# Threshold attention and an exact GELU MLP on one core: ten token blocks instead of eight by products of quarters, x^T copied by ScalarE and divided by GpSimd

## The chip, the cores and the metric

The kernel runs on one core of a Trainium2 chip. The engines of the core work side by side, each through its own list of instructions in order, and wait for one another by semaphores: TensorE (PE in the profile, with PEld for its weight loads) multiplies matrices into PSUM, VectorE (DVE) and ScalarE (ACT) work on tiles in SBUF and PSUM, GpSimd (POOL) works on tiles in SBUF and issues transfers, SyncE (SP) issues transfers. The metric is the time of one execution on the device in microseconds (us). Everything is float32; the weights arrive as 64-bit floats and are converted on the chip. What an engine computes is not changed by the edit beyond the order of some sums.

## The reference

There are 8 batches of 8 heads with 576 tokens of 64 elements. The attention keeps, in each row of scores, only those within tau of the row's maximum; a two-layer MLP follows.

```python
scores = scale * np.matmul(q, k.transpose(0, 1, 3, 2))
thresh = np.max(scores, axis=-1, keepdims=True) - tau
scores = np.where(scores >= thresh, scores, -1000000000.0)
scores = scores - np.max(scores, axis=-1, keepdims=True)
attn = np.exp(scores)
attn = attn / (np.sum(attn, axis=-1, keepdims=True) + 1e-09)
x = attn @ v                      # heads side by side: 4608 tokens x 512
h = x @ w_in                      # 512 x 2048
g = 0.5 * h * (1.0 + erf(h * inv_sqrt2))
out = g @ w_out                   # 2048 x 512
```

## The kernel before, in words

**Pairs and slots.** Two heads make a pair, four pairs a batch, 32 pairs in all. The 576 query rows of a pair are cut into four chunks of 128 rows for each of the two heads and a fifth chunk that holds the last 64 rows of both. One chunk is one slot: slots 0 to 3 of a pair have two score tiles (head 0 and head 1), slot 4 has one. Slots are numbered n = 0 to 159 through the kernel; the first 20 (the first batch) are done in another way and are not touched.

**One slot of the softmax.** `scores` (L358) has TensorE multiply q^T by k^T into a score tile in PSUM; the pool named sc has two such tiles, so that a slot with two tiles can only start when the slot before has let its own go. `softmax_head` takes the maximum with VectorE (L370, nmx), computes the threshold with GpSimd (L371, thr), and exponentiates with ScalarE (L373, p). `softmax_tail` has VectorE compare the score tile with the threshold, multiply, and sum the row (L389); this is the last reader of the score tile. `turn_p` (L436, L434) then has VectorE transpose p in 32x32 blocks, `regroup` has SyncE bring the blocks to their places in pT by DMA (L454, L458), and after slot 4 `divisors` inverts the row sums and has SyncE spread them over a tile named inv (L411 to L424).

**x^T.** In slot 2 of the next pair (`WEIGH = 2`) `weigh_v` multiplies v by p^T on TensorE into two tiles xT (L475, 20 matmuls in all), and VectorE multiplies xT by inv into a block of x, x_blk (L492). The function that does this, `divide`, is handed back to the main loop, which calls it for the first tile after `softmax_tail` and for the second after `turn_p`. In slot 2 VectorE also transposes q and k of the next pair (L340 to L346).

**The MLP as filling.** The 4608 tokens are 18 blocks of 256. A block done plainly (`block_steps`) is 64 matmuls of 256 columns for the first layer (hT, L549; after each eight, ScalarE applies GELU, L522, which needs a table load before it and one after it, L535, to get back to Exp) and 32 matmuls of 512 columns for the second (o_ps, L563). These matmuls are the filling that TensorE does in each slot behind the scores. How many go into a slot is fixed when the program is written out: `GOAL` gives the number of blocks that are to be done by certain slots, `PARTS = 1.2, 1.2, 0.8, 1.2, 0.6` shares it out over slots 0 to 4 of a pair, and `fill` emits matmuls until the debt is paid, from blocks whose tokens are ready (`tokens`).

**The blocks at the end.** The last 8 blocks are done two by two after the attention (`strassen`, L683): with seven products of quarters in place of eight, a duo of blocks takes 224 matmuls of 256 columns, where two plain blocks take 128 of 256 and 64 of 512 columns. VectorE makes the sums of quarters of w_in in `weights_in` (L623 to L631) and of x in `x_sums` (L649 to L652). Blocks that must wait for it and have no room in SBUF (`AWAY`) are written to DRAM by `put_away` and fetched by `bring`, both on SyncE's queue; the pool xg has seven buffers for blocks of x.

**GpSimd's list.** In slots 1 to 4 it holds, behind the slot's thr instructions, the issue of the loads of q, k and v of the pair after the next (four DMAs a slot, L224 and L233).

Of the kernel before, what the change touches and what calls it, by code (L numbers as in the profile page):

```python
# [8 lines left out]
FP32 = mybir.dt.float32  # L9
# [3 lines left out]
ALU = mybir.AluOpType  # L13
# [5 lines left out]
def kernel(  # L19
# [28 lines left out]
    nc = tc.nc  # L48
    ctx.enter_context(tc.manual_schedule())

    B, H, S, D = q.shape
    d_model, d_ff = moe_w_in.shape
    P = 128
    Q = 32
    HP = H // 2
    NP = B * HP
    EARLY = HP
# [6 lines left out]
    N_DM = d_model // P  # L64
    N_DF = d_ff // P
    TOK = 256
    N_BLK = B * S // TOK
    PLAIN = N_BLK - 8

    AWAY = [PLAIN, PLAIN + 1, PLAIN + 2]  # L70
    order = list(range(PLAIN + 3, N_BLK)) + AWAY
    DUOS = list(zip(order[0::2], order[1::2]))
    assert 2 * D == P and 2 * TAIL == P and HALF <= 512 and N_DM == HP and B * S % TOK == 0 and S % Q == 0 and TOK == 2 * P
    SLOTS = NC + 1
# [8 lines left out]
    xg = ctx.enter_context(tc.tile_pool(name="xg", bufs=7))  # L83
    op = ctx.enter_context(tc.tile_pool(name="op", bufs=2))
# [123 lines left out]
    st = {}  # L208
    x_blk = {}

    def load(p):
        for _ in load_steps(p):
            pass
# [135 lines left out]
    def scores(p, i):  # L349
        s = st[p]  # L350
        n = 1 if i == NC else 2
        sc = s["sc", i] = [ps.tile([P, 2, 512], FP32, tag="sc", name="sc", bufs=2) for _ in range(n)]
        for h in range(2):
            for e in range(n):
                rows = slice(0, P) if i == NC else slice(e * D, (e + 1) * D)
                lhsT = s["q_tail"] if i == NC else s["qT"][rows, i * P:(i + 1) * P]
                at = h * HALF + (TAIL if p < EARLY and e == 0 else 0)
                nc.tensor.matmul(  # L358
                    sc[e][:, h, 0:HALF], lhsT=lhsT, rhs=s["kT"][rows, at:at + HALF], start=True, stop=True)

    def softmax_head(p, i):

        s = st[p]
        n = len(s["sc", i])
        nmx = small.tile([P, 2], FP32, tag="nmx", name="nmx")
        thr = s["thr", i] = small.tile([P, 2], FP32, tag="thr", name="thr")
        w = s["p", i] = work.tile([P, 2 * S], FP32, tag="p", name="p")
        for e in range(n):
            sc = s["sc", i][e][:, :, 0:HALF]
            nc.vector.tensor_reduce(nmx[:, e:e + 1], sc, axis=AXIS.XY, op=ALU.max, negate=True)  # L370
            nc.gpsimd.tensor_scalar(  # L371
                thr[:, e:e + 1], nmx[:, e:e + 1], -1.0, tau_eff, op0=ALU.mult, op1=ALU.subtract)
            nc.scalar.activation(  # L373
                w[:, e * S:(e + 1) * S].rearrange("p (h s) -> p h s", h=2), sc, AF.Exp, bias=nmx[:, e:e + 1], scale=1.0)
# [64 lines left out]
    def by_64(t):  # L439
        return t.rearrange("p c s -> p (c s)").rearrange("p (g c s) -> p g c s", c=KR, s=2 * Q)  # L440
# [19 lines left out]
    def weigh_v(p, lo, hi):  # L460


        b, hp = divmod(p, HP)
        s = st[p]
        xT = ps.tile([P, 512], FP32, tag="mm", name="xT")
        for c in range(KR):
            for e in range(2):
                f = slice(e * D, (e + 1) * D)
                to = xT[f, 0:hi - lo]
                if p < EARLY:  # L470
                    rhs = s["pT"][0 if c == NC else e][:, c, lo:hi]
                else:
                    to = to.rearrange("p (g s) -> p g s", s=2 * Q)
                    rhs = by_64(s["pT"][e])[:, lo // (2 * Q):hi // (2 * Q), c, :]
                nc.tensor.matmul(  # L475
                    to, lhsT=s["v"][:, e, c, :], rhs=rhs, start=(c == 0), stop=(c == KR - 1))
        by = None if p < EARLY else s["inv"]
        if hi == S:
            del st[p]

        def divide():
            at = lo
            while at < hi:
                n, o = divmod(b * S + at, TOK)
                size = min(TOK - o, hi - at)
                if n not in x_blk:
                    x_blk[n] = xg.tile([P, N_DM, TOK], FP32, tag="x", name="x")
                to, x = x_blk[n][:, hp, o:o + size], xT[:, at - lo:at - lo + size]
                if by is None:
                    nc.scalar.copy(to, x)  # L490
                else:
                    nc.vector.tensor_tensor(to, x, by[:, at:at + size], op=ALU.mult)  # L492
                at += size

        if by is not None:
            return divide
        divide()


    NS_IN, NS_OUT = 4 * TOK / 2.4, 4 * d_model / 2.4  # L500
# [25 lines left out]
    def gelus_held():  # L526
        hold[0] = False
        while held:
            g, j, t = held.pop(0)
            gelu(g, j, t, t)  # L530
# [41 lines left out]
    def fill(ns, tokens):  # L572

        mlp["debt"] += ns
        while True:
            if mlp["next"] is None:
                n = mlp["n"]
                if n == PLAIN or (n + 1) * TOK > tokens:
                    break
# [32 lines left out]
    def weights_in():  # L612
# [13 lines left out]

        assert mlp["n"] == PLAIN and mlp["layer"] == 2
        for h in range(HF // U):
# [173 lines left out]
    BATCH = HP * SLOTS  # L802
    WIDE = 5 * 2 * Q
    WEIGH = 2
    START = 2 * HP + 2

    GOAL = [(-1, 0.0), (START - 1, 0.0), (BATCH - 1, 0.5)]
    GOAL += [(BATCH * (m + 2) + WEIGH, x) for m, x in enumerate([1.96, 3.3, 4.64, 5.98, 7.32, 8.66, PLAIN])]

    def goal(n):  # L810
        for (lo, x), (hi, y) in zip(GOAL, GOAL[1:]):
# [11 lines left out]
    loads = iter(())  # L823
    for n in range(len(slots) + WEIGH + 1):
        p, i = slots[n] if n < len(slots) else divmod(n, SLOTS)
        early = p < EARLY
        last = slots[n - 1] if 0 < n <= len(slots) else None
        if p < NP:
            scores(p, i)
            softmax_head(p, i)  # L830
        elif n == len(slots):
            ext = weights_in()
        gelus(0)
        if n == BATCH:
            gelus_held()
        table()
        made = []
        for args in due:
            weigh_v(*args)
        due = []  # L840
        if p > EARLY and i == WEIGH:
            made = [weigh_v(p - 1, lo, hi) for lo, hi in ((0, WIDE), (WIDE, S))]
        owed += (goal(n) - goal(n - 1)) * BLK_NS * (PARTS[i] if not early and p < NP else 1.0)
        if early:
            fill(owed, tokens)
            owed = 0.0
            table()
        if last and last[0] < EARLY and last[1] < NC:
            turn_p_early(*last)
        if p < NP:  # L850
            softmax_tail(p, i)
        if made:
            made[0]()
        if p < NP and not early:
            turn_p(p, i)
        if made:
            made[1]()
        if p < NP and not early:
            if i == 2:
                regroup(p, 1)  # L860
            if i > 2:
                regroup(p, i)
            if i == NC:
                divisors(p)
        if last and last[0] < EARLY and last[1] == NC:
            turn_p_early(*last)
        if p < HP - 1 and i == 0:
            turn_qk_early(p + 1)
            if p == 0:
                load_early(3)  # L870
                load_v_early(2)
                load_v_early(3)
            if p < 2:
                load_piece()
        if p < HP and i == NC and 0 < p < HP - 1:
            load(p + 3)
        if n == BATCH:
            for t in pd_tail + [turned_p[:, e, h, :, :] for e in range(2) for h in range(2)]:
                nc.gpsimd.memset(t[:, NB:4 * KR, :], 0.0)
        if p >= HP and i == 1 and p + 2 < NP:  # L880
            loads = load_steps(p + 2)
        if p >= HP:
            next(loads, None)
        if p >= HP and i == 1 and p + 1 < NP or p == HP - 1 and i == 2:
            scale_q(p + 1)
        if p >= HP - 1 and i == 2 and p + 1 < NP:
            turn_qk(p + 1)
        convert(3000 if n < 2 * HP else 3650 if n < BATCH - 1 else 1e9)
        if early:
            diagonal(p, i)  # L890
        if not early:
            lag[0] = 2 if p < NP else 0
            fill(owed, tokens)
            owed = 0.0
        if last and last[0] < EARLY:
            if last[1] == 1:
                due.append((last[0], 0, TOK))
            if last[1] == NC:
                due.append((last[0], TOK, S))
        if n == START - 1:  # L900
            tokens = TOK
        elif n == BATCH + 1:
            tokens = S
        elif p > EARLY and i == WEIGH and p % HP == 0:
            tokens = p // HP * S
            leaving += [n for n in AWAY if n in x_blk and (n + 1) * TOK <= tokens]
        elif leaving and i < 2:
            put_away(leaving.pop(0))
# [34 lines left out]
```

## Time and profile before

| | us |
|---|---|
| median of three runs (lowest, highest) | 1414.21 (1413.93, 1416.21) |
| the profiled execution, its span | 1413.93, 1412.1 |
| span up to slot 20, where the second batch starts | 150.84 |
| slots 20 to 158 | 848.63 |
| slot 159 up to the first product of quarters | 19.05 |
| the four duos of blocks and the last output | 393.58 |
| TensorE busy, of the span | 1377.0 |
| VectorE, ScalarE, GpSimd busy | 886.8, 636.3, 389.0 |

A row of the profile names the line of the kernel, the engine, the operation, what it writes and reads, and how many there were. In a row of a group the two numbers behind the bar are the time in which any of them ran and the mean of one in ns, and behind the next bar stands how long the engine had idled before them and for whom it waited. In a row of the timeline the first two numbers are the start and the length in us, and a bracket tells how long the engine idled before and who ended it. A float32 matmul shows as two records, so 128 records in a slot are 64 matmuls. TensorE's matmul records are lengthened by the pipeline; the distance between two weight loads tells the true pace.

### The profile page before, as it was taken

How to read it: one execution, taken by the hardware profiler on the slowest of the kernel's cores; microseconds unless marked ns; L12 is line 12 of the kernel's file. 1: busy time of each engine (PE TensorE's matmuls, PEld its weight loads, DVE VectorE, ACT ScalarE, POOL GpSimd, SP SyncE). 2: the span in 40 equal slices, each digit the busy share in tenths (PEclk: the TensorE clock that was granted, in tenths of full speed). 3: DMA queues.
4: the chain of work that ended last, by engine and by line, in shares of the span. 5: the costliest groups of instructions: out<-in, count | busy, mean ns of one | idle time of the engine just before them, and what ended most of it. 6: DMA issues, size and time to landing. Idle time of an engine off the chain costs nothing.

```text
span 1412.1 us, 19647 instructions
## 1 busy us (share of the span) xinstructions
PE 1377.0 (98%) x6544; PEld 956.6 (68%) x6544; DVE 886.8 (63%) x1772; ACT 636.3 (45%) x1052; POOL 389.0 (28%) x812
## 2 busy tenths in 40 slices
PE   6899899999999999999999999999999999999999
PEld 4677557466475564655746657466588888888887
DVE  5888687777777777777777777777664142241330
ACT  5766628445255373563745627447141140230320
POOL 4444244343344344344334344330000000000000
PEclk9999999999999999999999999999999999999999
DMA  9979267666666766666766776664400000001000
GB/s 259 294 276 261 68 140 154 134 150 127 141 150 135 162 131 140 143 146 150 164 132 145 164 158 143 148 140 100 108 1 8 23 1 26 19 1 51 9 8 23
DMA packets 219346, 167.05 MB, mean 118 GB/s; under 512 B 122480, under 2 KB 203952, under 8 KB 219248
## 3 DMA queue, kind: packets, MB, share of 16 engines
q1 hardware_dynamic: 193040, 108.65, 36.5%
q0 software_dynamic: 23808, 56.57, 13.1%
q8 instruction: 53, 0.87, 0.3%
q10 hardware_dynamic: 2400, 0.59, 0.2%
q14 instruction: 45, 0.37, 0.1%
HBM read 71.68 MB, written 11.47 MB: 59 GB/s over the span
## 4 chain that ended last, share of the span: by engine, by line
PE 91%; DVE 4%; ACT 3%; DMA 2%; issue 1%; SPq 0%; POOL 0%; DVEq 0%; ACTq 0%; POOLq 0%
PE bank L683 27%; PE hT L549 20%; PE o_ps L563 19%; PE sc L358 12%; PE xT L475 10%; PE tr L301 2%; DVE p L389 1%; ACT p L373 1%; DMA q<-in_q_dram 1%; DVE power L186 1%; DMA turned_p<-in_moe_w_in_dram 1%; DVE nmx L370 0%; DVE w_in L188 0%; ACT diag L403 0%; DVE power L178 0%
## 5 line engine op out<-in xcount | busy, mean ns | idle before, releaser
L373 ACT ACTIVATE p<-sc,nmx 128x576 f32<-128x576 f32 x288 | 202.1, 738 | 370.8 <-DVE nmx L370 370.6
L370 DVE TENSOR_REDUCE nmx<-sc 128x1 f32<-128x576 f32 x288 | 205.1, 749 | 163.1 <-PE sc L358 163.0
L563 PE MATMUL o_ps<-w_out,g 128*128 128x512 f32 x640 | 294.3, 602 | 3.0 <-ACT g L522 3.0
L549 PE MATMUL hT<-x,w_in 128*128 128x256 f32 x1280 | 296.1, 384 | 0.0
L549 PEld LDWEIGHTS hT<-x,w_in 128*128 128x128 f32 x1280 | 238.6, 190 | 56.0 <-issue 25.1
L389 DVE SCALAR_TENSOR_TENSOR p<-sc,thr,p 128x576 f32<-128x576 f32 x288 | 225.4, 816 | 65.1 <-ACT p L373 62.7
L371 POOL TENSOR_SCALAR thr<-nmx,tau_eff 128x1 f32<-128x1 f32 x288 | 84.1, 292 | 541.8 <-DVE nmx L370 541.8
L563 PEld LDWEIGHTS o_ps<-w_out,g 128*128 128x128 f32 x640 | 116.5, 190 | 142.6 <-issue 137.8
L358 PE MATMUL sc<-kT,qT 64*128 64x288 f32 x960 | 165.1, 437 | 1.4 <-DVE p L389 1.0
L475 PE MATMUL xT<-pT,v 128*64 128x256 f32 (+1 forms) x1280 | 163.7, 409 | 2.7 <-ACT g L522 2.7
L436 DVE STREAM_TRANSPOSE turned_p<-p 128x1152 f32<-128x1152 f32 x112 | 154.1, 1376 | 2.9
L358 PEld LDWEIGHTS sc<-kT,qT 64*128 64x128 f32 x960 | 93.4, 190 | 82.9 <-issue 70.3
L475 PEld LDWEIGHTS xT<-pT,v 128*64 128x64 f32 x1280 | 89.8, 137 | 74.0 <-issue 10.8
L233 POOL DMA_DIRECT2D v<-in_v_dram x208 | 110.5, 534 | 10.7 <-issue 9.8
L683 PE MATMUL bank<-x,w_in 128*128 128x256 f32 x384 | 93.3, 379 | 0.0
L683 PE MATMUL bank<-w_out,unit 128*128 128x256 f32 x416 | 92.4, 379 | 0.0
L522 ACT ACT_TABLE_LOAD x67 | 86.0, 1283 | 1.2
L535 ACT ACT_TABLE_LOAD x67 | 86.0, 1283 | 1.2
L683 PEld LDWEIGHTS bank<-w_out,unit 128*128 128x128 f32 x416 | 79.1, 190 | 10.7
L683 PEld LDWEIGHTS bank<-x,w_in 128*128 128x128 f32 x384 | 73.0, 190 | 10.3 <-issue 0.5
L224 POOL DMA_DIRECT2D q<-in_q_dram x104 | 70.7, 685 | 16.0 <-issue 15.1
L224 POOL DMA_DIRECT2D k<-in_k_dram x104 | 69.6, 675 | 0.7 <-DMA inv<-turned 0.3
(152 smaller groups left out, 1307.3 us busy)
## 6 DMA issues: line engine op xcount, KB each, us to landing
pT<-turned_p SPq DMA_DIRECT2D x448, 160.0 KB, 3.5
pT<-pd_tail SPq DMA_DIRECT2D x112, 80.0 KB, 2.9
q<-in_q_dram POOLq DMA_DIRECT2D x104, 72.0 KB, 4.1
k<-in_k_dram POOLq DMA_DIRECT2D x104, 72.0 KB, 2.6
inv<-turned SPq DMA_DIRECT2D x56, 128.0 KB, 3.9
v<-in_v_dram POOLq DMA_DIRECT2D x156, 40.0 KB, 3.2
out_dram<-o_sb SPq DMA_DIRECT2D x20, 256.0 KB, 4.3
raw<-in_moe_w_in_dram POOLq DMA_DIRECT2D x8, 512.0 KB, 5.6
```

Source lines behind the costliest of these rows:

```text
L224: eng.dma_start(t[e * D + f:e * D + f + Q], rows[:, :, f:f + Q])
L233: eng.dma_start(t[r:P:4, e, 0:n, :], rows[:, r * KR:r * KR + n, :])
L358: nc.tensor.matmul(sc[e][:, h, 0:HALF], lhsT=lhsT, rhs=s["kT"][rows, at:at + HALF], start=True, stop=True)
L370: nc.vector.tensor_reduce(nmx[:, e:e + 1], sc, axis=AXIS.XY, op=ALU.max, negate=True)
L373: nc.scalar.activation(w[:, e * S:(e + 1) * S].rearrange("p (h s) -> p h s", h=2), sc, AF.Exp, bias=nmx[:, e:e + 1], scale=1.0)
L389: nc.vector.scalar_tensor_tensor(row, sc[e][:, :, 0:HALF], thr[:, e:e + 1], row, op0=ALU.is_ge, op1=ALU.mult, accum_out=den[e])
L436: nc.vector.transpose(turned_p[:, :, i // 2, 0:NB, i % 2 * Q:(i % 2 + 1) * Q], w.rearrange("p (e b i) -> p e b i", e=2, i=Q))
L475: nc.tensor.matmul(to, lhsT=s["v"][:, e, c, :], rhs=rhs, start=(c == 0), stop=(c == KR - 1))
L522: nc.scalar.activation(t, src, AF.Gelu)
L549: nc.tensor.matmul(hT[:, j % 2, :], lhsT=w_in_sb[c][:, j * P:(j + 1) * P], rhs=x_blk[n][:, c, :], start=(c == 0), stop=(c == N_DM - 1))
L563: nc.tensor.matmul(o[:, 0:d_model], lhsT=g[j][:, m * P:(m + 1) * P], rhs=w_out_sb[j], start=(j == 0), stop=(j == N_DF - 1))
L683: nc.tensor.matmul(to, lhsT=l, rhs=r, start=start and k == 0, stop=k == len(pairs) - 1, skip_group_check=not start)
```

## The change

`PLAIN` goes from 10 to 8: ten blocks (five duos) instead of eight are left to the products of quarters, and two plain blocks fewer lie among the slots. Five blocks (8 to 12) instead of three are written to DRAM and fetched again. `GOAL` is set anew: about 1.01 blocks for each batch of 20 slots from the third batch on, in place of 1.34. `PARTS` stays as it is.

`weigh_v` no longer hands back a function: ScalarE copies xT to x_blk undivided as soon as the matmuls are done. A new function `divide` has GpSimd multiply the part of x_blk in place by inv, in slot 3 (`DIVIDE = 3`), behind the slot's thr instructions and ahead of the issue of the loads of v. The tokens of a batch count as ready one slot later. For the last pair the division follows the copies directly.

```diff
-    PLAIN = N_BLK - 8
-    AWAY = [PLAIN, PLAIN + 1, PLAIN + 2]
-    order = list(range(PLAIN + 3, N_BLK)) + AWAY
+    PLAIN = N_BLK - 10
+    AWAY = list(range(PLAIN, PLAIN + 5))
+    order = list(range(PLAIN + 5, N_BLK)) + AWAY
...
-        by = None if p < EARLY else s["inv"]
-        if hi == S:
-            del st[p]
-        def divide():
...
-                to, x = x_blk[n][:, hp, o:o + size], xT[:, at - lo:at - lo + size]
-                if by is None:
-                    nc.scalar.copy(to, x)
-                else:
-                    nc.vector.tensor_tensor(to, x, by[:, at:at + size], op=ALU.mult)
...
+        for n, o, at, size in in_blocks(b, lo, hi):
+            if n not in x_blk:
+                x_blk[n] = xg.tile([P, N_DM, TOK], FP32, tag="x", name="x")
+            nc.scalar.copy(x_blk[n][:, hp, o:o + size], xT[:, at - lo:at - lo + size])
+
+    def divide(p):
+        b, hp = divmod(p, HP)
+        by = st.pop(p)["inv"]
+        for n, o, at, size in in_blocks(b, 0, S):
+            x = x_blk[n][:, hp, o:o + size]
+            nc.gpsimd.tensor_tensor(x, x, by[:, at:at + size], op=ALU.mult)
...
+    DIVIDE = 3
-    GOAL += [(BATCH * (m + 2) + WEIGH, x) for m, x in enumerate([1.96, 3.3, 4.64, 5.98, 7.32, 8.66, PLAIN])]
+    GOAL += [(BATCH * (m + 2) + DIVIDE, x) for m, x in enumerate([1.96, 2.97, 3.98, 4.98, 5.99, 6.99])]
+    GOAL += [(BATCH * B + WEIGH, PLAIN)]
...
         if p > EARLY and i == WEIGH:
-            made = [weigh_v(p - 1, lo, hi) for lo, hi in ((0, WIDE), (WIDE, S))]
+            for lo, hi in (0, WIDE), (WIDE, S):
+                weigh_v(p - 1, lo, hi)
+            if p == NP:
+                divide(p - 1)
...
-        if made:
-            made[0]()
         if p < NP and not early:
             turn_p(p, i)
-        if made:
-            made[1]()
...
+        if EARLY < p < NP and i == DIVIDE:
+            divide(p - 1)
```

`in_blocks` cuts the 576 tokens of a pair at the borders of blocks, so that each division is three instructions; a copy, cut at the border of the two xT tiles too, is three or four.

More of the change, by code (lines that the diff above doesn't have):

```diff
@@ L476, in weigh_v, with in_blocks @@
                     to, lhsT=s["v"][:, e, c, :], rhs=rhs, start=(c == 0), stop=(c == KR - 1))
-        by = None if p < EARLY else s["inv"]
-        if hi == S:
-            del st[p]
-        def divide():
[L482 to L487, printed above, removed]
-                to, x = x_blk[n][:, hp, o:o + size], xT[:, at - lo:at - lo + size]
-                if by is None:
-                    nc.scalar.copy(to, x)
-                else:
[L492 to L497, printed above, removed]
+        for n, o, at, size in in_blocks(b, lo, hi):
+            if n not in x_blk:
+                x_blk[n] = xg.tile([P, N_DM, TOK], FP32, tag="x", name="x")
+            nc.scalar.copy(x_blk[n][:, hp, o:o + size], xT[:, at - lo:at - lo + size])
+    def in_blocks(b, lo, hi):
+        while lo < hi:
+            n, o = divmod(b * S + lo, TOK)
+            size = min(TOK - o, hi - lo)
+            yield n, o, lo, size
+            lo += size
+    def divide(p):
[4 more added lines that the diff above has]
+            nc.gpsimd.tensor_tensor(x, x, by[:, at:at + size], op=ALU.mult)
     NS_IN, NS_OUT = 4 * TOK / 2.4, 4 * d_model / 2.4
@@ L836 @@
         table()
-        made = []
         for args in due:
@@ L903 @@
             tokens = S
-        elif p > EARLY and i == WEIGH and p % HP == 0:
+        elif p > EARLY and i == DIVIDE and p % HP == 0 or p == NP and i == WEIGH:
             tokens = p // HP * S
```

## The prediction

> **What bounds the kernel now.** First the page's busy line and the chain that ended last:
>
> ```profile
> PE 1377.0 (98%) x6544; PEld 956.6 (68%) x6544; DVE 886.8 (63%) x1772; ACT 636.3 (45%) x1052; POOL 389.0 (28%) x812
> ...
> PE 91%; DVE 4%; ACT 3%; DMA 2%; issue 1%; SPq 0%; POOL 0%; DVEq 0%; ACTq 0%; POOLq 0%
> ```
>
> TensorE is the bound by both. An average hides stages, so next the windows of four stages (start, slots 20 to 158, slot 159, duos); the columns after the length are busy time of PE, PEld, DVE, ACT and POOL, the clock, the DMA share and GB/s:
>
> ```profile
> 0.00:150.84 150.84, 128.24 (x802) 97.72 (x803) 118.90 (x266) 96.54 (x206) 65.14 (x136) 0.98 0.86 259
> 150.84:999.47 848.63, 841.27 (x3877) 509.49 (x3876) 629.49 (x1185) 436.94 (x588) 323.57 (x675) 1.00 0.65 141
> 999.47:1018.52 19.05, 19.05 (x76) 9.16 (x75) 16.90 (x31) 1.10 (x2) 0.29 (x1) 1.00 0.56 117
> 1018.52:1412.10 393.58, 388.43 (x1794) 340.23 (x1792) 121.54 (x293) 101.68 (x258) 0.00 (x0) 1.00 0.05 16
> ```
>
> In the slots TensorE is busy 99% and VectorE 74%. But a slot is also a chain: scores, maximum, exponential, comparison, and only then the next scores. Whether it hides is seen in the timeline around slot 4 of a pair, here 938.72 to 942.15:
>
> ```profile
> 938.72 0.89 PEld L358 LDWEIGHTS sc<-kT,q_tail 128*128 128x128 f32 x4
> ...
> 940.11 0.76 DVE L370 TENSOR_REDUCE nmx<-sc 128x1 f32<-128x576 f32 x1 [1.31 <-PE sc L358]
> 940.90 0.74 ACT L373 ACTIVATE p<-sc,nmx 128x576 f32<-128x576 f32 x1 [4.52 <-DVE nmx L370]
> ...
> 941.74 0.82 DVE L389 SCALAR_TENSOR_TENSOR p<-sc,thr,p 128x576 f32<-128x576 f32 x1 [0.88 <-ACT p L373]
> 942.15 0.29 PEld L358 LDWEIGHTS sc<-kT,qT 64*128 64x128 f32 x2 [0.33 <-issue]
> ...
> 942.68 0.78 PEld L358 LDWEIGHTS sc<-kT,qT 64*128 64x128 f32 x6 [0.23 <-issue]
> ...
> 943.85 1.38 DVE L370 TENSOR_REDUCE nmx<-sc 128x1 f32<-128x576 f32 x2
> ```
>
> TensorE comes to slot 0 of the next pair at 942.15, loads two weights, and stops until 942.68, 0.12 after the comparison of slot 4 ended (942.56) and gave back the second score tile. So slot 4's chain already ends last, though the page calls the gap "issue". In the 27 pairs from slot 25 on, the maximum of slot 0 begins on average 1.65 us after its scores and not 1.27 as in a slot without this wait: 10.2 us in all. In slots 0 to 3 nothing waits: there TensorE needs 5.4 to 5.8 us with 10 matmuls, and VectorE gets from one maximum to the next in at least 4.65 (3.19 from maximum to the end of the comparisons, 1.46 to the end of the transpose).
>
> Last, the rows for prices:
>
> ```profile
> L371 POOL TENSOR_SCALAR thr<-nmx,tau_eff 128x1 f32<-128x1 f32 x288 | 84.1, 292 | 541.8 <-DVE nmx L370 541.8
> L106 POOL MEMSET v<- 128x640 f32 x4 | 2.3, 624 | 0.0
> L106 POOL MEMSET q_tail<- 128x128 f32 x4 | 0.6, 198 | 0.0
> L492 DVE TENSOR_TENSOR x<-xT,inv 128x128 f32<-128x128 f32 (+3 forms) x104 | 28.4, 312 | 6.4 <-PE xT L475 3.4 <-issue 1.3
> L490 ACT COPY x<-xT 128x256 f32<-128x256 f32 (+1 forms) x12 | 3.5, 327 | 0.7 <-PE xT L475 0.7
> ```
>
> **The change part by part.**
>
> *Matmuls.* Slot 3 with 10 hT matmuls is 5.38 long, with 11 it is 5.81: 0.43 each. Slot 2 with 3 o_ps is 8.94, with 4 it is 9.80: 0.86 each. A plain block is 64 x 0.43 + 32 x 0.86 = 55.0, two are 110.1. The duos start at 1018.52, 1116.20, 1213.68 and 1311.15 and so take 97.5. Moving two blocks saves 12.6 of TensorE's time: -110.1 among the slots, +97.5 behind them. Its weight sums cost nothing (made once), its x_sums and fetches lie beside matmuls as those of the four duos do.
>
> *What the slots give back.* The order of TensorE's instructions in both built programs says how much filling each slot loses. From slot 25 to 158, in us, slots 0 to 4 of all pairs: 119.5 to 96.3, 120.4 to 91.2, 77.4 to 61.9, 117.0 to 90.7, 57.6 to 45.1. What slot 4 loses, 12.5 or 0.46 a pair, is no gain: its chain was already the longer, so the wait in slot 0 grows by as much. Slot 3 falls to about 4.3 to 4.5, under VectorE's 4.65, so that slot 4's maximum starts up to 0.45 late (the transpose of slot 3 stands ahead of it); and where a GELU falls in slot 4, its two table loads (1.28 each, GELU 0.60) hold up the exponential of slot 0 by 0.3 to 0.5. I went through the slots one by one, each as long as the later of TensorE's filling and the chain (maximum +0.79 to the exponential, +0.84 to the comparison, +0.82 or +1.55 to its end, +0.12 to the next scores; ScalarE and VectorE free after the instructions that the order puts behind). For before this gives slot 159 at 995.3 where the trace has 999.5, waits of 9.3 (the trace's 10.2), and misses 3.3 in two slots (below); for the new order it gives waits of 29.6. Slots 0, 1 and 2 stay with TensorE (4.8 to 4.9, 8.1 to 8.9). So +20.3.
>
> *Two pauses.* Two slots 2 with 7 hT take 11.03 where others take 9.39: xT waits for PSUM, because two GELUs wait there. No slot 2 of the new order has two from the third batch on: -3.3. Bounds: ScalarE's copies now hold xT until about 9 us into slot 2 (behind exponentials, GELU and table load) where VectorE was done after 6.5; TensorE opens one new tile in that time, which the GELU's own buffer serves, so I take 0; were it to wait in each of some 14 pairs as in these two slots, +23.
>
> *VectorE's divisions* (28.4) go from slot 2, where TensorE's 8 to 9 us are the cover: 0. *ScalarE's copies*, 104 x 0.327 = 34, come into the same slot 2, where it has some 6 us of work: 0 while that cover stands. They are ahead of slot 3's exponentials, which start 10.6 after slot 2's scores; the copies end near 9. For a batch's first copies, those to a buffer that `put_away` empties wait for its DMA (512 KB, 4.7 us); with pairs 11% shorter this is tight in two or three slots, at most 1 us each; taken as 0.
>
> *GpSimd's divisions.* Three instructions in slot 3, 576 columns, ahead of four v loads (2.15) and of slot 4's thr. Counted from slot 3's maximum, thr ends at 1.81, +0.2, +2.15, + the divisions D, +0.29 for slot 4's thr: 4.51 + D with the hand-over. The comparison of slot 4 wants it at 4.65 + 1.63 = 6.28. So up to D = 1.77 it is free; above, slot 0's wait grows: 0.5 in all at 1.8, 2.4 at 1.9, 6.5 at 2.1, 10.8 at 2.3. No row shows D. MEMSET's slope is (624 - 198)/512 = 0.83 ns a column. Low end: one pass at that slope and three starts of 0.1 = 0.8. High end: three passes (two reads, a write) and thr's 0.29 three times = 2.3. I take two passes, one for each operand read, with thr's start, the one arithmetic row: 1.83, +1.0.
>
> *A rule that speaks against it.* The Trainium skill, GPSIMD Engine Reference, section 4.1, says to keep two-input elementwise work on VectorE, GpSimd being about twice as slow; section 3.1 puts it at 2.6 cycles an element at 1.2 GHz. By that alone 576 columns are an estimated 1.25 us and cost nothing here; with thr's measured start three times, 2.1, and the sum would be 5.5 us higher. No run here shows it yet.
>
> *SyncE's queue.* In slots 78 to 82 p^T's last pieces land at 527.3 (issued 521.5 to 524.4, 2.9 to land) and are read at 533.6; the stretch between shortens by about 2.9, so 3.4 remain; two more put_aways (0.7 each to issue) stand behind these. 0.
>
> *The end.* Slot 159 has 12 o_ps instead of 15 (in the 110.1). TensorE would reach the first product 2.6 earlier, but its second product reads x that VectorE's third x_sum ends only 17.95 after slot 159's scores: +0.7.
>
> Sum, against the profiled execution's 1413.93 (0.02% under the median): -110.1 + 97.5 + 20.3 - 3.3 + 1.0 + 0.7 = +6.1, so 1420.0.
>
> **The rivals.** (1) *The divisions hold up thr*: D of 2.1 to 2.3 makes it 1425.5 to 1430, D of 3 (+27.6) 1447. For: GpSimd is the one engine whose price is unseen, and the margin is nil. Against: 28% busy. (2) *The waits don't grow*: the full saving, 1413.93 - 110.1 + 97.5 - 3.3 + 0.7 = 1398.7. It needs slot 4's chain to be hidden; it decides for faster when the growth stays under 11.4 us, 0.42 a pair, below even the 0.46 taken from slot 4. The 27 waits at slot 0 speak against it. (3) *PSUM or DMA*: xT held by ScalarE, or p^T late by 1 us in each pair: +23 to +27, 1443 to 1447.
>
> **How the numbers follow.** Forecast (1415 to 1425, the slot account's miss of 4 us either way) 0.62; rival 1 0.22; rival 2 0.08; rival 3 0.08. The range from 1414 to 1435 leaves out rival 2, D above 2.5 and most of rival 3. What a measurement can tell from no change is 0.2%, 2.8 us: faster 0.08, within 0.12 (the low edge of the forecast), slower 0.80.
>
> **What would show it.** The wait of slot 0's second score tile at about 1.1 us a pair instead of 0.4; TensorE's busy share in the slots down by 2 to 3%; five duos of 97.5; slot 159 near 911. D as the three GpSimd rows, and whether slot 4's comparison waits for thr. Wrong if slot 0's wait is near 0.4, or if the pairs take over 27.5 us (30.4 before; 27.0 by this account).

## The result, and the profile after

The changed kernel takes 1422.41 us (median of four runs, 1421.36 to 1423.81) where the kernel before takes 1414.90 on the same chip (1413.93 to 1416.21): a ratio of 1.0053 with a 95% interval of 1.0036 to 1.0071. It is slower by 7.5 us. The profiled execution took 1421.36, its span is 1419.5. One execution of eight_pool below, 1602.36 us at a mean clock of 0.849 where the others have 0.994 to 0.998, fell in a slower state of the chip and is left out of that run's numbers.

First the page of the kernel after: the busy line, and the chain that ended last by engine.

```profile
PE 1375.2 (97%) x6608; PEld 970.4 (68%) x6608; DVE 888.3 (63%) x1734; ACT 636.8 (45%) x1164; POOL 433.9 (31%) x896
...
PE 80%; DVE 10%; ACT 7%; issue 1%; DMA 1%; SPq 1%; ACTq 0%; DVEq 0%
```

TensorE is busy 1.8 us less than before, and its share of the chain has fallen from 91% to 80%: VectorE (10%, 4% before) and ScalarE (7%, 3% before) have taken the place. So something else became the bound in part of the time. The busy time does not show the 12.6 us of matmuls that were saved, as records stretched by waits or a lower clock count as busy; the stages show it, and where the loss lies. The windows of the kernel after, with the columns of the prediction's table:

```profile
0.00:148.67 148.67, 125.85 (x802) 95.79 (x802) 118.73 (x266) 96.33 (x206) 65.35 (x136) 0.99 0.87 262
148.67:910.96 762.29, 746.92 (x3500) 440.94 (x3499) 602.98 (x1082) 412.23 (x633) 365.70 (x756) 1.00 0.71 156
910.96:928.45 17.49, 17.08 (x70) 8.35 (x69) 16.16 (x29) 1.60 (x4) 0.73 (x2) 1.00 0.70 150
928.45:1419.50 491.05, 485.39 (x2242) 425.33 (x2240) 150.41 (x360) 126.65 (x322) 2.08 (x3) 1.00 0.05 17
```

The slots from 20 to 158 take 762.29 instead of 848.63, the duos 491.05 instead of 393.58. In the slots TensorE was idle 848.63 - 841.27 = 7.4 us before and is idle 762.29 - 746.92 = 15.4 us now, in a shorter stretch; its busy share there fell from 99.1% to 98.0%. The span grew by 7.4:

| stage | before | after | difference |
|---|---|---|---|
| up to slot 20 (code not touched) | 150.84 | 148.67 | -2.2 |
| slot 20 | 10.42 | 13.06 | +2.6 |
| slots 21 to 158 | 838.21 | 749.23 | -89.0 |
| slot 159 to the first product | 19.05 | 17.49 | -1.6 |
| the duos (four, then five) | 393.58 | 491.05 | +97.5 |

Within slots 21 to 158 the matmuls taken out are worth -107.6, and the two pauses in slot 2 are gone (-3.3); the waits gave back some 21. The wait is seen in the timeline around a slot 4 of the kernel after (slot 99) and slot 0 of the next pair. The columns are start, length, engine, line and operation; the bracket is the idle time before it and who ended it.

```profile
590.75 0.76 DVE L370 TENSOR_REDUCE nmx<-sc 128x1 f32<-128x576 f32 x1
...
591.54 0.74 ACT L373 ACTIVATE p<-sc,nmx 128x576 f32<-128x576 f32 x1 [2.04 <-DVE nmx L370]
...
592.35 0.29 PEld L358 LDWEIGHTS sc<-kT,qT 64*128 64x128 f32 x2 [0.76 <-issue]
...
592.38 0.82 DVE L389 SCALAR_TENSOR_TENSOR p<-sc,thr,p 128x576 f32<-128x576 f32 x1 [0.88 <-ACT p L373]
...
593.32 0.78 PEld L358 LDWEIGHTS sc<-kT,qT 64*128 64x128 f32 x6 [0.68 <-issue]
...
594.49 0.72 DVE L370 TENSOR_REDUCE nmx<-sc 128x1 f32<-128x576 f32 x1
```

TensorE loads the first two weights of slot 0 at 592.35, while VectorE has not even begun slot 4's comparison. The other six weights come at 593.32, 0.12 after the comparison ended (593.20) and gave the second score tile back. The two loads stood 0.53 apart in the prediction's timeline and are 0.97 apart here. Here too the row of the weight load has "issue", but the view of what TensorE's matmuls waited for (who, for whom: total, times, longest) names the comparison. Its row in the kernel before:

```profile
PE sc L358 <- DVE p L389: 1.5, 5, 0.5
```

Its row in the kernel after:

```profile
PE sc L358 <- DVE p L389: 12.2, 26, 0.9
```

These totals are smaller than the waits themselves, because the records of the matmuls ahead are stretched into them; a wait is better measured by how late the maximum comes. Summed as in the prediction, over the 27 pairs from slot 25 on, the lateness of slot 0's maximum went from 10.2 to 28.9 us, 0.38 to 1.07 a pair; in slots 1 and 2 it went from 0 to 2.6, and slot 4's maximum is late by 6.5 in place of 1.9.

### The profile page after: what moved, and what is told of

Same layout as the page of the kernel before. It is cut to its first block, busy times and chain, and to the rows that moved or that the text cites. A ratio compares the mean times of both kernels' runs of the same rounds, so it can differ in the third digit from the quotient of the medians.

```text
span 1419.5 us, 19992 instructions
## 1 busy us (share of the span) xinstructions
PE 1375.2 (97%) x6608; PEld 970.4 (68%) x6608; DVE 888.3 (63%) x1734; ACT 636.8 (45%) x1164; POOL 433.9 (31%) x896
## 4 chain that ended last, share of the span: by engine, by line
PE 80%; DVE 10%; ACT 7%; issue 1%; DMA 1%; SPq 1%; ACTq 0%; DVEq 0%
PE bank L680 34%; PE hT L546 12%; PE o_ps L560 11%; PE sc L358 11%; PE xT L475 10%; DVE p L389 4%; ACT p L373 3%; DVE nmx L370 2%; PE tr L301 2%; DVE turned_p L436 1%; ACT L519 1%; ACT L532 1%; DVE power L186 1%; DVE w_in L188 1%; DMA q<-in_q_dram 0%
## 5 line engine op out<-in xcount | busy, mean ns | idle before, releaser
L560 PE MATMUL o_ps<-w_out,g 128*128 128x512 f32 x512 | 241.1, 610 | 3.0 <-ACT g L519 3.0
L546 PE MATMUL hT<-x,w_in 128*128 128x256 f32 x1024 | 241.1, 385 | 0.0
L546 PEld LDWEIGHTS hT<-x,w_in 128*128 128x128 f32 x1024 | 189.6, 190 | 50.1 <-issue 25.3
L358 PE MATMUL sc<-kT,qT 64*128 64x288 f32 x960 | 175.4, 436 | 12.6 <-DVE p L389 12.2
L560 PEld LDWEIGHTS o_ps<-w_out,g 128*128 128x128 f32 x512 | 93.5, 192 | 113.8 <-issue 108.6
L680 PE MATMUL bank<-x,w_in 128*128 128x256 f32 x480 | 116.7, 379 | 0.0
L680 PE MATMUL bank<-w_out,unit 128*128 128x256 f32 x520 | 115.5, 379 | 0.0
L680 PEld LDWEIGHTS bank<-w_out,unit 128*128 128x128 f32 x520 | 98.8, 190 | 13.4
L680 PEld LDWEIGHTS bank<-x,w_in 128*128 128x128 f32 x480 | 91.2, 190 | 12.8 <-issue 0.5
L680 PE MATMUL bank<-v,unit 128*128 128x256 f32 x320 | 82.1, 379 | 0.0
L680 PE MATMUL bank<-unit,turned_p 128*128 128x256 f32 x320 | 73.1, 379 | 0.0
```

The source lines that it names most:

```text
L358: nc.tensor.matmul(sc[e][:, h, 0:HALF], lhsT=lhsT, rhs=s["kT"][rows, at:at + HALF], start=True, stop=True)
L546: nc.tensor.matmul(hT[:, j % 2, :], lhsT=w_in_sb[c][:, j * P:(j + 1) * P], rhs=x_blk[n][:, c, :], start=(c == 0), stop=(c == N_DM - 1))
L560: nc.tensor.matmul(o[:, 0:d_model], lhsT=g[j][:, m * P:(m + 1) * P], rhs=w_out_sb[j], start=(j == 0), stop=(j == N_DF - 1))
L680: nc.tensor.matmul(to, lhsT=l, rhs=r, start=start and k == 0, stop=k == len(pairs) - 1, skip_group_check=not start)
```

## The experiments

The time of the kernel before, on the chip of the runs, was 1414.90 us beside the changed kernel, 1416.29 beside the next four rows, and 1416.23 beside the last four; each ratio is to its own. "Slot-0 wait" is the lateness just described, from the profiled execution.

| kernel | blocks in duos | slot 4's share | divisions on | slot-0 wait, us | time, us | ratio to before, 95% interval |
|---|---|---|---|---|---|---|
| before | 8 | 0.6 | VectorE | 10.2 | | 1 |
| after | 10 | 0.6 | GpSimd | 28.9 | 1422.41 | 1.0053 (1.0036 to 1.0071) |
| ten_even | 10 | 1.05 | GpSimd | 0.6 | 1396.93 | 0.9867 (0.9851 to 0.9882) |
| ten_less4 | 10 | 0.3 | GpSimd | 54.3 | 1457.87 | 1.0286 (1.0257 to 1.0316) |
| eight_even | 8 | 0.75 | VectorE | 0.7 | 1405.59 | 0.9924 (0.9901 to 0.9948) |
| ten_vector | 10 | 0.6 | VectorE | 32.0 | 1437.92 | 1.0146 (1.0121 to 1.0171) |
| ten_mid | 10 | 0.8 | GpSimd | 13.2 | 1410.68 | 0.9963 (0.9950 to 0.9977) |
| ten_even_vector | 10 | 1.05 | VectorE | 5.4 | 1422.79 | 1.0042 (1.0027 to 1.0057) |
| eight_pool | 8 | 0.6 | GpSimd | 9.8 | 1417.41 | 1.0006 (0.9996 to 1.0016) |
| ten_div4 | 10 | 0.6 | GpSimd, one twice | 36.7 | 1432.63 | 1.0115 (1.0100 to 1.0130) |

The theory (A) is the prediction's: slot 4 has too little filling, its chain ends last, and each matmul taken from slot 4 comes back as a wait at slot 0. The first rival (B) puts the loss on the divisions and copies that moved to GpSimd and ScalarE. A third theory (C) has the five duos cost more than they save, wherever the other matmuls lie.

**Filling moved into slot 4 (ten_even).** The number of matmuls is that of the changed kernel; only their shares over slots 0 to 4 are others, above all slot 2's (0.45 for 0.8) and slot 4's.

```diff
-    PARTS = 1.2, 1.2, 0.8, 1.2, 0.6
+    PARTS = 1.15, 1.15, 0.45, 1.2, 1.05
```

> The changed kernel with PARTS = 1.15, 1.15, 0.45, 1.2, 1.05: same matmuls, but slot 4 gets 1.05 of a share of the filling instead of 0.6, and slot 2 0.45 instead of 0.8. Theory A (slot 4's chain outlasts its filling, and what is taken from slot 4 comes back as a wait in slot 0): the wait at slot 0 falls from 1.0 to about 0.1 us a pair, slot 159 starts near 885 instead of 911, and the time is 1396 to 1399, faster than the kernel before. Theory B (the divisions on GpSimd hold up the thresholds): the placing of the matmuls doesn't matter, 1422 within 3. Theory C (the five duos cost more than they save, in whatever place): 1422 within 3.

Measured: 1396.93 us (1395.66 to 1399.35), 19 faster than the kernel before and some 26 faster than the changed one. The slot-0 wait is 0.6 us. The page's busy line and chain, one window of slots 22 to 158, and the timeline around a slot 4 of ten_even:

```profile
PE 1362.8 (98%) x6608; PEld 968.8 (69%) x6608; DVE 890.1 (64%) x1734; ACT 640.8 (46%) x1167; POOL 433.2 (31%) x896
...
PE 93%; DVE 2%; DMA 2%; ACT 2%; issue 1%; POOL 0%; SPq 0%; ACTq 0%; DVEq 0%; POOLq 0%
```

```profile
173.49:887.91 714.42, 713.68 (x3433) 429.20 (x3433) 595.22 (x1065) 402.64 (x610) 361.00 (x742) 1.00 0.75 166
```

```profile
580.76 0.82 DVE L389 SCALAR_TENSOR_TENSOR p<-sc,thr,p 128x576 f32<-128x576 f32 x1 [0.88 <-ACT p L373]
...
581.59 0.89 PEld L358 LDWEIGHTS sc<-kT,qT 64*128 64x128 f32 x8 [0.76 <-issue]
...
582.87 1.41 DVE L370 TENSOR_REDUCE nmx<-sc 128x1 f32<-128x576 f32 x2
```

TensorE is idle for 0.7 us in 714, and the eight weights of slot 0 load in one go: the comparison (ended 581.58) has just let the tile go when TensorE arrives. The VectorE, ScalarE and GpSimd work is the same as in the changed kernel, so the loss did not lie in it. This speaks for A, and against B and C, which both had 1422.

**Less filling in slot 4 (ten_less4).** The same line, in the other direction.

```diff
-    PARTS = 1.2, 1.2, 0.8, 1.2, 0.6
+    PARTS = 1.3, 1.3, 1.0, 1.1, 0.3
```

> The changed kernel with PARTS = 1.3, 1.3, 1.0, 1.1, 0.3: slot 4 gets half of its share, the others more. Theory A: each us taken from slot 4 is lost, 0.3 of a share is 0.86 us in each of 27 pairs; the wait at slot 0 grows from 1.0 to about 2.0 us a pair, and the time is 1442 to 1446. Theories B and C: 1422 within 3.

Measured: 1457.87 us (1450.74 to 1460.15). The slot-0 wait was 54.3, 2.0 a pair, as expected; the time was 12 above the upper end. What was missing from the account is the clock. The timeline of TensorE's weight loads of ten_less4 at one such wait, and six windows of 1 us behind it (the third column from the end is the granted clock):

```profile
443.40 0.29 PEld L358 LDWEIGHTS sc<-kT,qT 64*128 64x128 f32 x2 [0.33 <-issue]
...
445.75 0.78 PEld L358 LDWEIGHTS sc<-kT,qT 64*128 64x128 f32 x6 [2.05 <-issue]
```

```profile
446.40:447.40 1.00, 1.00 (x6) 0.59 (x4) 0.93 (x5) 0.98 (x2) 0.08 (x1) 1.00 0.95 206
447.40:448.40 1.00, 1.00 (x4) 0.80 (x4) 0.90 (x2) 0.99 (x3) 0.30 (x2) 0.56 0.96 273
448.40:449.40 1.00, 1.00 (x4) 0.82 (x3) 0.54 (x1) 0.99 (x2) 0.28 (x1) 0.50 0.80 242
449.40:450.40 1.00, 1.00 (x4) 0.73 (x4) 1.00 (x4) 0.00 (x0) 0.00 (x0) 0.50 0.91 174
450.40:451.40 1.00, 1.00 (x5) 0.86 (x4) 0.97 (x3) 0.00 (x0) 0.00 (x0) 0.73 0.94 186
451.40:452.40 1.00, 1.00 (x7) 0.84 (x5) 0.43 (x1) 0.00 (x0) 0.00 (x0) 1.00 0.84 130
```

After a pause of 2.05 us the clock is granted at half for 3.41 us, from 447.52 on. The profiled execution has three such spells behind waits at slot 0; the slots that they fall in take 8.63 to 9.28, where those with as many matmuls mostly take 7.16 to 7.38. That is some 5 us of its 1450.74, and without them it would lie at the upper end of what was expected. The other three runs show a lower mean clock (0.986 to 0.988, not 0.993) and took 1456.8 to 1460.2. So direction and waits agree with A, and its time left out a second price of long waits. That the remaining distance of the other runs is more of the same spells is argued from their mean clock; there is no trace of them.

**The same in the kernel before (eight_even).**

```diff
-    PARTS = 1.2, 1.2, 0.8, 1.2, 0.6
+    PARTS = 1.15, 1.15, 0.75, 1.2, 0.75
```

> The kernel before (eight blocks, divisions on VectorE) with PARTS = 1.15, 1.15, 0.75, 1.2, 0.75 alone. Theory A: its own wait of 0.38 us a pair at slot 0 goes, and the time falls by 8 to 10 to 1404 to 1407; ten blocks with an even filling should then be faster than this by 7 to 10, most of the 12.6 that two blocks save. Theory C: ten blocks with an even filling no faster than this.

Measured: 1405.59 us (1401.36 to 1408.98), the slot-0 wait 0.7 instead of 10.2, as expected. So an even filling alone is worth 10.7 to the kernel before, and 19 is not what ten blocks bring. Two kernels without this wait can now be compared: ten blocks against eight is 1396.93 - 1405.59 = -8.7 us, of the 12.6 that the matmuls alone are worth. They differ in the engine of the divisions too, but VectorE waits for inv in eight_even for no more than 0.1 us in all, and with eight blocks the move was worth nothing (eight_pool, below).

**An intermediate share (ten_mid).**

```diff
-    PARTS = 1.2, 1.2, 0.8, 1.2, 0.6
+    PARTS = 1.15, 1.15, 0.7, 1.2, 0.8
```

> The changed kernel with PARTS = 1.15, 1.15, 0.7, 1.2, 0.8, between the change (0.6 in slot 4) and the even filling (1.05). Theory A: the wait at slot 0 is halved, to about 0.5 us a pair, and the time is 1408 to 1411, half way. Were the gain of the even filling due to slot 2's smaller share, or to one threshold: near 1397 or near 1422.

Measured: 1410.68 us (1407.30 to 1415.48), the slot-0 wait 13.2. With the others this gives a row of four: slot 4's share 0.3, 0.6, 0.8 and 1.05; waits of 54.3, 28.9, 13.2 and 0.6 us; times of 1457.9, 1422.4, 1410.7 and 1396.9, which are 41.6 and 7.5 above and 5.6 and 19.4 below the kernel before on the same chip. From 0.6 to 0.8 the wait falls by 15.7 and the time by 13.1; from 0.8 to 1.05 the wait falls by 12.6 and the time by 13.8. So the time follows the wait nearly one to one; between 0.3 and 0.6 it moves by more than the wait (34.1 for 25.4), and there the clock has its part. Slot 2's share moves against slot 4's in all four kernels, so that the times alone do not tell the two apart; that it is slot 4 is read from the traces, where the wait stands at slot 0, behind slot 4's comparison.

**The divisions back on VectorE (ten_vector).** The changed kernel with its ten blocks and its order of TensorE's instructions, but `weigh_v` and the main loop as before.

```diff
-            nc.scalar.copy(x_blk[n][:, hp, o:o + size], xT[:, at - lo:at - lo + size])
+                    nc.vector.tensor_tensor(to, x, by[:, at:at + size], op=ALU.mult)
...
-        if EARLY < p < NP and i == DIVIDE:
-            divide(p - 1)
+        if made:
+            made[0]()
```

> The changed kernel with the divisions of x^T back on VectorE, straight from PSUM, as in the kernel before; TensorE's order is the same, instruction by instruction. Theory A: VectorE has 2 us to spare in slot 2, so nothing moves beyond the 0.5 us that I put on GpSimd's divisions: 1420 to 1423. Theory B: back to 1414 or below.

Measured: 1437.92 us (1434.50 to 1440.56). Neither theory had this: without the move the ten blocks cost 14 us more (21.6 over the kernel before on the same chip, not 7.5), not nothing. The views of VectorE's waits (who was waited for: total, times, longest) and of the timeline of ten_vector show why:

```profile
DVE x L492 <- DMA inv<-turned: 30.4, 15, 3.8
```

```profile
393.84 0.57 SPq L416 DMA_DIRECT2D turned<-turned  x1
...
397.01 0.60 SPq L422 DMA_DIRECT2D inv<-turned  x1
...
398.96 0.61 SPq L424 DMA_DIRECT2D inv<-turned  x1
...
402.98 0.56 DVE L492 TENSOR_TENSOR x<-xT,inv 128x128 f32<-128x128 f32 x2 [3.57 <-DMA inv<-turned]
...
406.88 1.42 DVE L370 TENSOR_REDUCE nmx<-sc 128x1 f32<-128x576 f32 x2
```

The inverse row sums go to DRAM and come back in five transfers on SyncE's queue. From the issue of the first (393.84) to the landing of the last (about 402.9) it is 9 us. Over the pairs of all ten profiles it is 7.0 to 11.2, and on average 8.4 to 8.9 in each, so it does not shrink with the pair: inv lands on average 3.4 after slot 2's scores in the kernel before, and 6.3 after them here. VectorE comes to the division at 399.4 and stands there for 3.57; behind it wait the transposes and the maximum of the next slot, which begins 3.85 after its scores where 1.27 is usual. In the kernel before, whose pairs are 2.7 us longer (30.2 against 27.5), VectorE never waits for inv at this line. About 5 us between the runs of ten_vector go with the mean clock: two runs with a mean of 0.996 took 1434.5 and 1435.3, two with 0.991 and 0.992 took 1440.5 and 1440.6.

**Even filling with the divisions on VectorE (ten_even_vector).** Both edits together; D is the theory that inv comes late for VectorE in short pairs, E that it doesn't once the filling is even.

```diff
-    PARTS = 1.2, 1.2, 0.8, 1.2, 0.6
+    PARTS = 1.15, 1.15, 0.45, 1.2, 1.05
...
-            nc.scalar.copy(x_blk[n][:, hp, o:o + size], xT[:, at - lo:at - lo + size])
+                    nc.vector.tensor_tensor(to, x, by[:, at:at + size], op=ALU.mult)
```

> Ten blocks with the even filling (1396.9) and the divisions back on VectorE in slot 2. Theory D (in slot 2 VectorE waits for the inverses to land, 30.4 us in the run with the divisions on VectorE, and the shorter the pair the longer the wait): pairs are shorter still, so it is slower than the even filling by 12 or more, 1409 to 1425, with idle time before the divisions put down to the DMA of inv. Theory E (VectorE's own 28 us of divisions are what costs, and only where slot 2 is tight): 1399 to 1403, with little idle time there.

Measured: 1422.79 us (1419.01 to 1423.57), so D. The view of VectorE's waits of ten_even_vector:

```profile
DVE x L492 <- DMA inv<-turned: 27.0, 17, 4.0
```

With even filling, having GpSimd divide is worth 1422.79 - 1396.93 = 25.9 us.

**The division's move alone, with eight blocks (eight_pool).** The kernel before with ScalarE's copies and GpSimd's divisions in slot 3.

```diff
-                    nc.vector.tensor_tensor(to, x, by[:, at:at + size], op=ALU.mult)
+            nc.scalar.copy(x_blk[n][:, hp, o:o + size], xT[:, at - lo:at - lo + size])
...
+            nc.gpsimd.tensor_tensor(x, x, by[:, at:at + size], op=ALU.mult)
```

> The kernel before (eight blocks, its own filling) with the copies on ScalarE and the divisions on GpSimd alone. Theory D: pairs of 30.4 us leave the inverses time to land, so there is no wait to take away: within 2 of the kernel before. Theory E: part of the 14 us that separate the two ten-block kernels, 1406 to 1411.

Measured: 1417.41 us (1415.18 to 1418.61), ratio 1.0006 (0.9996 to 1.0016): no difference. In pairs of 30.3 us inv is there in time, and the work that VectorE is rid of (863.0 us busy on the page, 886.8 before) is worth nothing.

**A longer division (ten_div4).** The changed kernel with one division of 256 columns done a second time, so that D, the time of GpSimd's divisions in a slot 3, grows by one such row.

```diff
-        for n, o, at, size in in_blocks(b, 0, S):
+        parts = list(in_blocks(b, 0, S))
+        more = [t for t in parts if t[3] == TOK][:1]
+        for n, o, at, size in parts + more:
```

> The changed kernel with one division of 256 columns done twice (0.73 us more on GpSimd in slot 3 of each pair; x is divided twice there, so the output is another). Theory A with its margin for GpSimd (D = 1.77 free, 1.79 measured): D becomes 2.52, slot 4's comparison waits for thr, the wait at slot 0 grows by 0.6 us a pair: 1436 to 1441. If the margin isn't real: 1422 within 2.

Measured: 1432.63 us (1430.38 to 1433.80), between the two. The view of VectorE's waits of ten_div4, and its timeline:

```profile
DVE p L389 <- POOL thr L371: 29.5, 26, 1.4
```

```profile
592.79 2.38 POOL L496 TENSOR_TENSOR x<-x,inv 128x256 f32<-128x256 f32 x4
...
595.11 2.15 POOL L233 DMA_DIRECT2D v<-in_v_dram  x4
597.30 0.31 POOL L371 TENSOR_SCALAR thr<-nmx,tau_eff 128x1 f32<-128x1 f32 x1
...
597.65 0.82 DVE L389 SCALAR_TENSOR_TENSOR p<-sc,thr,p 128x576 f32<-128x576 f32 x1 [1.26 <-POOL thr L371]
```

The chain of the first rival is real: divisions, then the issue of four loads of v, then thr, then the comparison. VectorE's 1.26 here has to be held against the 0.88 that it waits for the exponential in the changed kernel, so the true loss is near 0.4 in this pair. Over all pairs the slot-0 wait grows by 7.8 us, 0.29 a pair. The prediction's formula, nothing free above D = 1.77, would have lost twice that (the 0.6 expected), so the margin is an estimated 0.3 to 0.4 larger than reckoned.

## Why the prediction was right

The forecast was 1420.0 against 1413.93 for the profiled execution before, +6.1; the profiled executions differ by 7.4, the medians by 7.5. By its own steps:

- **Matmuls.** The five duos took 97.48 each (they start at 928.45, 1026.13, 1123.61, 1221.09 and 1318.56), and slot 159 began at 910.96 where the account had 911. Right.
- **What the slots give back**, +20.3 from a growth of 9.3 to 29.6. Measured is some 21: 18.7 at slot 0, 2.6 in slots 1 and 2, where the account had none. The sign follows from the share: 12.5 us of filling were taken from a slot whose chain already ended last. ten_even shows it as the cause: give slot 4 its filling, and the wait and the loss are gone. One sign did not come: TensorE's busy share in the slots was to fall by 2 to 3% and fell by 1.1, as its stretched records cover part of each wait. The second rival (1398.7, the waits don't grow) was refuted for this kernel, and ten_even reached its number with another sharing.
- **Two pauses**, -3.3. No slot 2 from the third batch on is 11.03 long any more. Right; and the third rival, late PSUM or p^T, is not in the trace, where TensorE's matmuls wait 0.4 us for xT in all.
- **GpSimd's divisions**, +1.0 with D = 1.83. The rows of the changed kernel, by shape:

```profile
L494 POOL TENSOR_TENSOR x<-x,inv 128x256 f32<-128x256 f32 x40 | 28.6, 727 | 0.0
L494 POOL TENSOR_TENSOR x<-x,inv 128x192 f32<-128x192 f32 x16 | 9.5, 593 | 0.0
L494 POOL TENSOR_TENSOR x<-x,inv 128x128 f32<-128x128 f32 x16 | 7.3, 456 | 0.0
L494 POOL TENSOR_TENSOR x<-x,inv 128x64 f32<-128x64 f32 x12 | 4.2, 352 | 15.2 <-DMA inv<-turned 15.2
```

  Two of 256 and one of 64 make 0.727 + 0.727 + 0.352 = 1.81: D was right as a sum of rows, and it lies just above the 1.77. But it cost nothing: VectorE waited for thr four times, 1.7 us in all (five times, 2.3, in the kernel before). The rows overlap: in 24 of the 25 pairs whose divisions are followed by loads of v, the issue of v starts 1.63 to 1.65 after the divisions began, and by 1.64 the prediction's own formula has them free. So the term of +1.0 was mis-sized, and the margin is larger still by what ten_div4 shows. The first rival was not in this kernel. The 15.2 in the last row is one wait, behind the last pair, where GpSimd has nothing else to do.
- **The end**, +0.7. The stretch from slot 159 to the first product is 1.56 shorter, with three o_ps of 0.86 taken out: -2.58 + 1.0. Right within 0.3. That the total came within 1.3 owes something to luck: the 1.0 of the divisions that did not come stood against about 1 that the waits took beyond the account.
- **VectorE's divisions**, 0, covered by TensorE's 8 to 9 us in slot 2. The value was right for this sum (eight_pool: no difference), and the cover named was not the whole condition. The divisions were free before because inv, too, had landed. In pairs of 27.5 us it lands late, and with the divisions left on VectorE the ten blocks cost 14 us more (ten_vector). The step asked what VectorE's work costs, and not what the same instruction would wait for after the pairs had become shorter. So the move to GpSimd did have an effect in this change: it kept a second wait away.
- **What the sum did not have.** Slot 20 took 2.6 longer, the code before it 2.2 less; they nearly cancel, and neither comes from the change. Slot 20 begins between 148.67 and 153.62 in the ten profiles of this study, whose code up to there is the same. And it takes 10.42 only in the profile of the kernel before; in the nine others, eight_pool with the same filling among them (13.40), it takes 12.1 to 14.3. The reason is the clock, below.

## What to carry to other kernels

Where the matmuls of one stage are the filling of another stage's chain, the number of matmuls is half of the question and their sharing over the slots the other half: a matmul taken where the chain already ends last is no gain. After such a change the shares are set anew; here the old shares turned a saving of 12.6 us into a loss of 7.5, and other shares make it 19 faster than before, of which 10.7 were to be had without the change. And when a period becomes shorter, look at the transfers whose length doesn't shrink with it, and at what is queued behind the first engine that reads them.

## What was not expected of the hardware

- **A short pause can halve the clock, and where it falls counts.** In slot 20 of the kernel after TensorE waited 3.24 us for a GELU. The timeline of its weight load, and the windows around it:

```profile
154.61 0.50 PEld L560 LDWEIGHTS o_ps<-w_out,g 128*128 128x128 f32 x2 [3.24 <-ACT g L519]
```

```profile
148.67:152.00 3.33, 2.77 (x20) 1.85 (x18) 2.67 (x6) 2.16 (x5) 0.83 (x5) 1.00 0.02 5
152.00:156.50 4.50, 1.89 (x3) 0.86 (x4) 2.53 (x5) 4.47 (x8) 0.51 (x4) 0.62 0.01 2
156.50:160.00 3.50, 3.50 (x6) 1.44 (x5) 0.00 (x0) 3.48 (x8) 0.00 (x0) 0.51 0.00 0
```

  The clock is at half from 153.1 on for 6.83 us, and the slot takes 2.6 longer than in the profile of the kernel before, which shows as much idle time there (TensorE busy 7.24 of 10.42) at full clock. The other eight profiles have the half clock in slot 20 too. In ten_less4 three of the 27 waits at slot 0 were followed by 3.41 us at half; in the kernel after, whose waits are shorter, none was, and in ten_vector and ten_div4 one each.
  The clock's record tells more of when. In each of the ten profiles all spells at half begin at multiples of 3.413 us from one another, within 0.003 (49 spells in all), so each trace can be laid out in windows of 3.413 us. From 30 us into the program on, up to its last two windows, the share of a window at full clock that TensorE's matmul records cover goes with what the next window is granted:

  | covered | windows at full clock | of them followed by half clock |
  |---|---|---|
  | under 40% | 20 | 20 |
  | 40 to 50% | 12 | 9 |
  | 50 to 60% | 26 | 8 |
  | 60 to 70% | 35 | 1 |
  | over 70% | 3914 | 0 |

  So the same pause can cost something or nothing by where it falls in these windows. The pause of slot 20 falls across two of them: they are covered 51% and 56% in the kernel after and 55% and 52% in the kernel before, in the band in which both are seen. What decides there, the traces do not show.
  The Trainium skill, TensorE: Matmul & The Clock Gate, Part 1, says that the clock falls to half after an idle window of about 3.4 us, and that the windows run freely. The windows found here agree with free-running ones; that windows in which TensorE was busy for a third to a half of the time were enough does not agree with a whole idle window, and there the measurement decides.
- **The price of a two-input product on GpSimd.** By the rows above it is (727 - 456)/128 = 2.12 ns a column of 128 partitions and 0.456 - 128 x 0.00212 = 0.19 us to start.
  The Trainium skill, GPSIMD Engine Reference, section 3.1, has 2.6 cycles an element at 1.2 GHz, which is an estimated 2.17 ns; the trace agrees. Its advice in section 4.1 to leave such work to VectorE did not hold in this kernel: VectorE would have been quicker at it (0.19 to 0.43 us an instruction in the kernel before, where GpSimd's rows take 0.35 to 0.73), and would have had to wait for inv (ten_vector, ten_even_vector).
- **What stays open.** No run moves a pause within its window, so that the place of a pause as the cause of half clock is read from the traces and not tried; nor was it tried whether a sharing better than that of ten_even exists. Of the 12.6 us that ten blocks save in matmuls, 8.7 were measured between the two even kernels. By their traces some 3 of the other 3.9 lie in slots 25 to 158, which are that much longer in ten_even than its fewer matmuls make them, and about 1 behind slot 159's start, the prediction's term for the end; why the slots are longer stays open.
